# The next pair's queries and keys: load written one tile later and in two transfers

## Chip, cores, metric

One core of one Trainium2 chip. The metric is the device time in microseconds (us) of one execution. The kernel before takes 540.03 us, the median of 3 runs (539.34 to 540.26).

## What is computed

Attention over 4 batches, 8 heads, 576 positions and head width 64, with a rotary turn of queries and keys, and then a mixture of experts in which every token goes to one of 8 experts:

```python
q_rot, k_rot = rotate(q), rotate(k)          # x1*cos - x2*sin, x1*sin + x2*cos
scores = scale * np.matmul(q_rot, k_rot.transpose(0, 1, 3, 2))
attn = softmax(scores)
x = np.matmul(attn, v)                       # tokens of 8*64 = 512
logits, local_gate = x @ w_gate, sigmoid(x @ w_local)
# e = argmax(logits), or the previous token's e when local_gate >= 0.5
h = np.maximum(x[b, s] @ w1[e], 0.0)
out[b, s] = p[e] * (h @ w2[e])
```

## The kernel before, in words

The attention runs over 16 pairs of heads (4 batches with 4 pairs each). A pair has 9 tiles of 128 score rows, so there are 144 steps `g`; `p, i = divmod(g, 9)`. In step `g` TensorE makes the scores of tile `g + 1` (`s`, L266), VectorE takes the minimum of a row (`mn`, L271), ScalarE the exponential (`e`, L288), TensorE turns an earlier tile (`tm` and, for the ninth tile, `tt`), and ScalarE and VectorE split the turned tile into a high and a low part (`pth`, `ptl`). For the pair before, TensorE sums up the values (`pv`, L363). The ninth tile of a pair, made first from pair 2 on, reads `qtail`; the other eight read `qst` and `m`.

What a pair needs is prepared some pairs ahead, on GpSimd (POOL) and by transfers that SyncE (SP) issues:

- `load_qk(p)` (L186 to L188) brings the queries and keys of a pair, each with its turned copy, into `qkl`: four planes of 576 columns, the first two queries, the last two keys. There is one such buffer. From pair 4 on it is written in the program at `i == 0` of pair `p - 3`, behind `rope(p - 1)`, which reads the buffer's earlier contents.
- `rope` (L195, L196): for keys and then for queries, one product with the table, in place, and one sum into `rr`.
- `split_qk` (L205, L206): `rr` is split into `xq` and `xk`, from which SP spreads the pair (`spread`): two transfers of `qtail` (L233), six of `m` (L220 to L222) and four of `qst` (L228), 12 in all, written at `i == 0` ahead of `rope`.
- `split_v` (L211, L212) and `load_v` (L192) do the same for the values.
- Behind each pair come its rows: TensorE multiplies the finished pair with the gate's weights and turns it (`gx`, L437, in two groups), ScalarE and POOL (L444, L450, L451), and for the second group VectorE (L450, L451), scale it into `xrow`, and three row stores (`store`, L461 and L465) bring it to `rows_d` in DRAM, which only the experts read. They are popped from the list `soon` at the end of a step, the stores at `i == 0`, behind `load_qk` in the program.

Buffers that bear on this: `gx` and `pv` share the four PSUM buffers of `ps_t`; `xrow` and the ninth tile's exponentials `et` share the four SBUF buffers of `et_p`, so each of them becomes free when the store has landed, or when `tt` has read it.

From step 12 on TensorE's order is the written one, and a planner puts the instructions of the other engines in order when the program is built, by the order written and by when it reckons that each can go. SP issues in that fixed order, too. Behind the attention, routing and experts follow; all of the first expert work is on the same engines.

Of the kernel before, what the change touches and what calls it, by code (L numbers as in the profile page):

```python
# [136 lines left out]
def tile_attention_moe(ctx, tc, qk, v, tabs, turn, consts, tri, wg, wts, out):  # L137
    nc = tc.nc
    pe, act, dve, pool, sp = nc.tensor, nc.scalar, nc.vector, nc.gpsimd, nc.sync
# [33 lines left out]
    qkl = stage[:, 0:2304].rearrange("p (f s) -> p f s", f=4)  # L173
# [9 lines left out]
    NPAIR = B * NP  # L183
    PASSES = ((0, 0), (0, 1), (1, 0))

    def load_qk(p):  # L186
        b, hp = divmod(p, NP)
        sp.dma_start(qkl, qk[b, hp])  # L188

    def load_v(p):  # L190
        b, hp = divmod(p, NP)
        sp.dma_start(vl[p % 2], v[b, hp])  # L192

    def rope_half(engine, f, x):
        engine.tensor_tensor(x, x, tab[:, 2 * f:2 * f + 2], op=ALU.mult)  # L195
        engine.tensor_tensor(rr[:, f], x[:, 0], x[:, 1], op=ALU.add)  # L196
# [5 lines left out]
    def split_qk(p):  # L202
        parts = [(xq, rr)] if p % 2 == 0 else [(xk[1], rr[:, 1]), (xq[:, :, 0], rr[:, 0])]
        for x, src in parts:
            pool.tensor_scalar(x[:, 0], src, 1.0, 1.0, op0=ALU.mult, op1=ALU.mult)  # L205
            pool.tensor_tensor(x[:, 1], src, x[:, 0].bitcast(F32), op=ALU.subtract)  # L206

    def split_v(p):
        v2 = v2_p.tile([P, 10, 2, D], F32R, tag="v2", name=f"v2_{p}")
        src = vl[p % 2]  # L210
        pool.tensor_scalar(v2[:, :, 0], src, 1.0, 1.0, op0=ALU.mult, op1=ALU.mult)  # L211
        pool.tensor_tensor(v2[:, :, 1], src, v2[:, :, 0].bitcast(F32), op=ALU.subtract)  # L212
        v2_t[p] = v2
# [21 lines left out]
    def spread(p):  # L235
        spread_tail(p)
        spread_k(p)
        spread_q(p)
# [109 lines left out]
    def pv_mm(p, n):  # L348
        u, n = divmod(n, 10)
        h, a = divmod(u, 2)  # L350
        k, hl = divmod(n, 2)
        if n == 0:
            pv_t[p, u] = ps_t.tile([P, HALF], F32, tag="t", name=f"pv_{p}_{u}")
        v2 = v2_t[p]
        hs = slice(h * HALF, (h + 1) * HALF)
        if k < 4:
            lhs = v2[:, 4 * a + k]
            rhs = (pthi, ptlo)[hl][p][:, a, k, hs]
        else:

            lhs = v2[:, 8 + a]
            rhs = (pkhi, pklo)[hl][p][:, hs]
        pe.matmul(pv_t[p, u], lhs.rearrange("p c d -> p (c d)"), rhs, start=(n == 0), stop=(n == 9))  # L363
# [837 lines left out]
    if True:  # L1201
        begin = ExitStack()
        begin.enter_context(tc.manual_schedule())
        raw = pt_p.tile([P, 2, 4, S], F32, tag="pt", name="raw")
        with tc.manual_schedule():
            rest_q, keep_awake, pair_1 = first_pair()
        sp.dma_start(wid, wg)
        load_v(0)
        sp.dma_start(tab[:, 3], tabs[:, 3])
        sp.dma_start(raw[:, 1], qk[0, 2])  # L1210
        sp.dma_start(tab[:, 0:2], tabs[:, 0:2])
        load_v(1)
        sp.dma_start(cst, consts)
        sp.dma_start(trif, tri)

        sp.dma_start(rows_d[0:1], zrow)

        def rope_2():
            for f in (1, 0):
                rope_half(pool, f, raw[:, 1, 2 * f:2 * f + 2])  # L1220

        NSTEP = NPAIR * 9
        soon, todo, minima = [], [], {}
        START = {
            0: [lambda: split_v(0)], 1: [rest_q[1], lambda: keep_awake(1)], 2: [rest_q[2], lambda: load_qk(3)],
            3: [pair_1[0], pair_1[1], rope_2, lambda: split_qk(2)], 4: [pair_1[2]], 5: pair_1[3:5],
            6: pair_1[5:6], 7: pair_1[6:8] + [lambda: split_v(1), lambda: load_v(2)],
            8: [lambda: spread(2)], 40: [lambda: act.copy(trib, trif)],
        }


        cum = [0, *itertools.accumulate(PV_STEPS)]

        def pv_steps(t):
            p, i = divmod(t, 9)
            if 0 <= p < NPAIR:
                for n in range(cum[i], cum[i + 1]):
                    pv_mm(p, n)
                    if n % 10 == 9:
                        pv_evac(p, n // 10)  # L1240

        for g in range(NSTEP):
            if g == GM:
                begin.close()
            with tc.manual_schedule(engines=None if g < GM else MAN0):
                p, i = divmod(g, 9)
                if i == 0 and p % NP == 0:
                    b = p // NP
                    sum_t[b] = sm_p.tile([P, H * NB], F32, tag="sum", name=f"sum_{b}")
                    dve.memset(sum_t[b], 1.0)  # L1250
                mn = minima.pop(g) if g in minima else softmax_min(g)
                if g == 0:
                    rest_q[0]()
                if g + 1 < NSTEP:
                    mm_s(g + 1)
                softmax_exp(g, mn)
                if g < GM - 1:
                    minima[g + 1] = softmax_min(g + 1)
                if g >= 2:
                    tr_main(g - 2)  # L1260
                pv_steps(g - 11)

                if i == 0 and 2 <= p and p + 2 < NPAIR or g == SPREAD_LAST:
                    spread(p + 1)
                if g in START:
                    for f in START[g]:
                        f()
                if i == 0 and 1 <= p and p + 2 < NPAIR:
                    rope(p + 2)
                    if p + 3 < NPAIR:  # L1270
                        load_qk(p + 3)
                if i == 5 and 1 <= p and p + 3 < NPAIR:
                    split_qk(p + 2)
                if g == QK_LAST:
                    split_qk(NPAIR - 1)
                if i == 3 and 1 <= p and p + 1 < NPAIR:
                    split_v(p + 1)
                    if p + 2 < NPAIR:
                        load_v(p + 2)

                if i == GATES_AT.get(p, 7) and p >= 2:
                    soon += gates(p - 2)
                    if (p - 2) % NP == NP - 1:
                        soon.append(lambda b=(p - 2) // NP: scores(b))
                        if (p - 2) // NP == B - 2:
                            todo += route(0, B - 1)
                if soon:
                    soon.pop(0)()
                f = todo.pop(0) if todo else None
                if f:  # L1290
                    list(f())
        moe = experts_phase()
        with tc.manual_schedule(engines=MAN1):
            last = NPAIR - 1
            held = []

            def tail_of(p):
                for n in range(cum[(NSTEP - 12) % 9 + 1], 40):
                    pv_mm(p, n)
                    if n % 10 == 9:  # L1300
                        pv_evac(p, n // 10)

            def pv_unit(u):
                for n in range(10):
                    pv_mm(last, 10 * u + n)
                pv_evac(last, u)

            def first_experts():
                for t in range(1, KE):
                    expert_of(t)  # L1310
                for k in range(2):
                    load_w(1, k)

            def rest_of_w():
                for k in range(LOAD0, 8):
                    load_w(0, k)

            drain = {
                "s": soon, "t": [lambda f=f: list(f()) for f in todo if f], "P": [lambda: tail_of(last - 1)],
                "w": [rest_of_w], "a": [lambda: tr_main(NSTEP - 2)], "b": [lambda: tr_main(NSTEP - 1)],  # L1320
                "g": gates(last - 1), "e": [first_experts], "S": [lambda c=c: split_w(0, c) for c in (1, 2, 3)],
                "u": [lambda u=u: pv_unit(u) for u in range(4)], "x": [lambda: held.append(turn_x(0, True))],
                "G": gates(last), "X": [lambda: held[0]()],
            }
            for c in DRAIN:
                if drain[c]:
                    drain[c].pop(0)()
            assert not any(drain.values())
        with tc.manual_schedule(engines=MAN2):
            side["parts"] = itertools.chain.from_iterable(f() for f in route(B - 1, 1))  # L1330
            for t in moe:
                pe_slot()
                if t == MANUAL:
                    break
        with tc.manual_schedule():
            for t in moe:
                pass
        rest_phase()
# [59 lines left out]
```

## Time and profile before

| | |
|---|---|
| median of 3 runs | 540.03 us |
| the profiled execution | 539.95 us |
| its span, first to last instruction | 538.2 us |
| TensorE matmul busy | 516.9 us (96%) |
| TensorE weight load busy | 458.4 us (85%) |
| VectorE busy | 381.0 us (71%) |
| ScalarE busy | 347.3 us (65%) |
| GpSimd busy | 341.0 us (63%) |
| mean rate of all transfers | 181 GB/s |

The shares are averages over unlike stages. Pairs 2 to 13 of the attention run from about 42 to 243 us, the last pairs with the routing to about 306 us, and the experts from there to about 520 us. In a row of the timeline the first number is the start, the second the duration, and a bracket at its end tells how long the engine had been idle and what ended that.

### The profile page before, as it was taken

The numbers are of one execution on the slowest core, as the hardware profiler recorded it, in microseconds if no ns is written. First come the engines' busy times: TensorE is split into PE (matmuls) and PEld (weight loads), VectorE is DVE, ScalarE is ACT, GpSimd is POOL, SyncE is SP. The second block draws the span as 40 slices with busy tenths as digits, with TensorE's granted clock in tenths as the row PEclk, the third lists the DMA queues.
The fourth block names the chain that finished last, engine by engine and source line by source line (L and its number), as shares of the span: only waits on it lengthen the run. The fifth ranks groups of instructions, "written<-read, shape, count | busy, mean of one in ns | idle before, by whom it ended". The sixth has DMA issues, their size and how long they took to land.

```text
span 538.2 us, 10733 instructions
## 1 busy us (share of the span) xinstructions
PE 516.9 (96%) x3273; PEld 458.4 (85%) x3273; DVE 381.0 (71%) x693; ACT 347.3 (65%) x766; POOL 341.0 (63%) x272
## 2 busy tenths in 40 slices
PE   7998999999999999998989999999999999999993
PEld 4888999999999999998879788887888887888882
DVE  6998999999999999999998845537412746421731
ACT  4988999999999999988776523353433443532440
POOL 4998999979969999896698302346411455411332
PEclk9999999999999999999999999999999999999998
DMA  8659799797996979977378205462537395637350
GB/s 289 265 131 230 197 232 235 186 213 201 221 225 145 230 203 231 222 189 166 57 209 223 76 21 176 148 245 71 205 117 236 98 372 130 223 100 235 82 175 26
DMA packets 63610, 97.34 MB, mean 181 GB/s; under 512 B 28145, under 2 KB 38897, under 8 KB 61746
## 3 DMA queue, kind: packets, MB, share of 16 engines
q1 hardware_dynamic: 60066, 86.45, 59.1%
q0 software_dynamic: 3040, 9.71, 5.6%
q8 instruction: 28, 0.46, 0.4%
q14 instruction: 44, 0.36, 0.2%
q10 hardware_dynamic: 432, 0.36, 0.2%
HBM read 76.95 MB, written 12.86 MB: 167 GB/s over the span
## 4 chain that ended last, share of the span: by engine, by line
PE 80%; DVE 8%; ACT 4%; issue 4%; POOL 2%; DMA 1%; SPq 0%; ACTq 0%; POOLq 0%; DVEq 0%
PE h L959 18%; PE o L1002 17%; PE pv L363 14%; PE s L266 13%; PE tm L324 10%; PE gx L437 3%; DVE mn L271 2%; PE th L993 2%; PE tx L945 1%; ACT e L288 1%; DVE ptl L306 1%; PE tk L334 1%; DVE w L904 1%; DMA turn<-in_turn_dram 1%; ACT w L901 1%
## 5 line engine op out<-in xcount | busy, mean ns | idle before, releaser
L1002 PE MATMUL o<-w,hs 128*128 128x512 f32 x456 | 113.4, 398 | 0.0
L271 DVE TENSOR_REDUCE mn<-s 128x1 f32<-128x576 f32 x144 | 107.2, 745 | 2.3 <-PE s L266 0.9
L959 PE MATMUL h<-w,xs 128*128 128x512 f32 x444 | 106.2, 393 | 0.8 <-DVE xs L306 0.5
L288 ACT ACTIVATE e<-s,mn 128x576 f32<-128x576 f32 x128 | 95.4, 745 | 15.9 <-DVE mn L271 13.3
L306 DVE TENSOR_TENSOR ptl<-tm,pth 128x512 fp32r<-128x512 f32 x139 | 95.4, 687 | 13.4 <-ACT pth L302 8.9
L1008 POOL DMA_INDIRECT out_dram<-os,sidx x19 | 23.1, 1214 | 126.5 <-ACTq L910 85.0
L266 PE MATMUL s<-m,qst 128*128 128x288 f32 x512 | 96.3, 310 | 5.7 <-ACT e L288 4.8
L959 PEld LDWEIGHTS h<-w,xs 128*128 128x128 f32 x444 | 82.5, 188 | 19.1 <-DVE w L904 1.1
L1002 PEld LDWEIGHTS o<-w,hs 128*128 128x128 f32 x456 | 83.0, 188 | 17.4 <-DVE hs L984 0.4
L302 ACT CAST pth<-tm 128x512 fp32r<-128x512 f32 x139 | 80.8, 582 | 10.6 <-PE tm L324 9.6
L266 PEld LDWEIGHTS s<-m,qst 128*128 128x128 f32 x512 | 74.1, 188 | 10.0 <-ACT e L288 7.5
L363 PE MATMUL pv<-pth,v 128*128 128x288 f32 x256 | 76.6, 315 | 1.3 <-DVE ex_row L702 0.4
L324 PE MATMUL tm<-wid,e 128*128 128x128 f32 x512 | 77.0, 272 | 0.0
L363 PE MATMUL pv<-ptl,v 128*128 128x288 f32 x256 | 76.3, 314 | 0.0
L195 POOL TENSOR_TENSOR stage<-stage 128x1152 f32<-128x1152 f32 x26 | 69.2, 2670 | 3.0 <-DMA stage<-in_qk_dram 2.9
L324 PEld LDWEIGHTS tm<-wid,e 128*128 128x128 f32 x512 | 62.2, 140 | 0.7 <-DVE ptl L306 0.3
L904 DVE TENSOR_TENSOR w<-stage,w 128x1024 fp32r<-128x1024 f32 x37 | 50.6, 1403 | 14.6 <-ACT w L901 9.7
L363 PEld LDWEIGHTS pv<-pth,v 128*128 128x128 f32 x256 | 48.3, 189 | 3.6 <-issue 2.5
L363 PEld LDWEIGHTS pv<-ptl,v 128*128 128x128 f32 x256 | 48.3, 189 | 0.0
L306 DVE TENSOR_TENSOR xs<-tx,xs 128x512 fp32r<-128x512 f32 x19 | 13.1, 689 | 42.7 <-ACTq L910 32.9
L196 POOL TENSOR_TENSOR stage<-stage 128x576 f32<-128x576 f32 x26 | 37.1, 1434 | 0.3
L306 DVE TENSOR_TENSOR hs<-th,hs 128x512 fp32r<-128x512 f32 x26 | 17.5, 687 | 27.7 <-ACTq L910 16.2
(201 smaller groups left out, 821.3 us busy)
## 6 DMA issues: line engine op xcount, KB each, us to landing
stage<-in_wts_dram SPq DMA_DIRECT2D x84, 512.0 KB
stage<-in_qk_dram SPq DMA_DIRECT2D x13, 1152.0 KB
qst<-xq SPq DMA_DIRECT2D x56, 128.0 KB
stage<-in_v_dram SPq DMA_DIRECT2D x16, 320.0 KB
m<-xq SPq DMA_DIRECT2D x14, 288.0 KB
m<-xk SPq DMA_DIRECT2D x14, 288.0 KB
m<-xq SPq DMA_DIRECT2D x14, 256.0 KB
m<-xk SPq DMA_DIRECT2D x14, 256.0 KB
```

What stands on the lines that cost most here:

```text
L195: engine.tensor_tensor(x, x, tab[:, 2 * f:2 * f + 2], op=ALU.mult)
L196: engine.tensor_tensor(rr[:, f], x[:, 0], x[:, 1], op=ALU.add)
L266: pe.matmul(st[:, h, lo:hi], lhs, keys[:, k0:k0 + hi - lo], start=(n == 0), stop=(n == len(parts_) - 1))
L271: dve.tensor_reduce(mn, s_t[g][:, :, 0:HALF], axis=AX.XY, op=ALU.min)
L288: act.activation(dst.rearrange("p (h s) -> p h s", h=2), s_t.pop(g)[:, :, 0:HALF], AF.Exp, bias=mn, scale=-1.0, accum_out=sums[:, col:col ...
L302: act.copy(hi, src)
L306: dve.tensor_tensor(lo, src, hi.bitcast(F32), op=ALU.subtract)
L324: pe.transpose(ps[:, k], src[:, k * P:(k + 1) * P], ident)
L363: pe.matmul(pv_t[p, u], lhs.rearrange("p c d -> p (c d)"), rhs, start=(n == 0), stop=(n == 9))
L904: (pool if k in on_pool else dve).tensor_tensor(lo, src, hi.bitcast(F32), op=ALU.subtract)
L959: pe.matmul(ps[:, c], xs_t[t][:, x, k], w[y][:, c * 512:(c + 1) * 512], start=(k == 0 and n == 0), stop=(k == 3 and n == 2))
L1002: pe.matmul(ps, hs_t[t][:, x, k], w[y][:, (k % 2) * 512:(k % 2 + 1) * 512], start=(k == 0 and n == 0), stop=(k == 7 and n == 2))
```

## The change

`load_qk` issues two transfers in place of one, the two planes of the keys first and then those of the queries, and from pair 4 on the call stands at `i == 1` in place of `i == 0`. As the row stores are popped at the end of step `i == 0`, the load is now behind them in the program. The load of pair 3, in step 2, stays where it is and is two transfers too.

```diff
     def load_qk(p):
         b, hp = divmod(p, NP)
-        sp.dma_start(qkl, qk[b, hp])
+        for f in (1, 0):
+            sp.dma_start(qkl[:, 2 * f:2 * f + 2], qk[b, hp, :, 2 * f:2 * f + 2])
...
                 if i == 0 and 1 <= p and p + 2 < NPAIR:
                     rope(p + 2)
-                    if p + 3 < NPAIR:
-                        load_qk(p + 3)
+                if i == 1 and 1 <= p and p + 3 < NPAIR:
+                    load_qk(p + 3)
                 if i == 5 and 1 <= p and p + 3 < NPAIR:
                     split_qk(p + 2)
```

## Rows read from the trace of the kernel before

**Rows 1.** Busy time by stretch: length, PE, PEld, DVE, ACT, POOL, PEclk, DMA share, GB/s

```profile
0.00:13.50 13.50, 10.42 (x43) 6.28 (x44) 9.03 (x27) 5.65 (x13) 6.24 (x10) 1.00 0.86 288
...
102.80:119.50 16.70, 16.70 (x133) 16.51 (x132) 15.83 (x32) 15.51 (x41) 13.68 (x11) 1.00 0.92 215
...
169.60:186.30 16.70, 16.57 (x131) 16.09 (x131) 15.46 (x30) 15.37 (x39) 16.38 (x16) 1.00 0.96 227
...
253.10:280.00 26.90, 24.91 (x184) 22.15 (x182) 26.30 (x61) 20.18 (x48) 19.78 (x30) 1.00 0.56 117
```

**Rows 2.** Chain that ended last, first scores of a pair: start, us, what

```profile
108.59 0.80 PE s L266 x6
...
124.97 0.80 PE s L266 x6
...
141.34 0.80 PE s L266 x6
...
158.04 0.80 PE s L266 x6
...
224.85 0.80 PE s L266 x6
```

**Rows 3.** TensorE's weight loads: one idle time, and the waits from 137 to 236 us

```profile
149.22 0.19 PEld L363 LDWEIGHTS pv<-pth,v 128*128 128x128 f32 x1 [0.33 <-issue]
...
PEld pv L363 <- issue: 1.6, 5, 0.3
PEld tm L324 <- DVE ptl L306: 1.2, 6, 0.2
PEld pv L363 <- POOL v L211: 0.3, 1, 0.3
```

**Rows 4.** Timeline ahead of that idle time, VectorE and TensorE

```profile
145.77 0.18 DVE L450 TENSOR_TENSOR gm<-gx,sum 128x36 f32<-128x36 f32 x1
...
148.32 0.27 PE L340 MATMUL tt<-wid,et 128*128 128x128 f32 x1
...
148.69 0.41 DVE L451 TENSOR_TENSOR xrow<-gx,sum 128x256 f32<-128x256 f32 x1
```

**Rows 5.** The same two VectorE instructions two pairs earlier

```profile
113.03 0.18 DVE L450 TENSOR_TENSOR gm<-gx,sum 128x36 f32<-128x36 f32 x1
113.13 0.41 DVE L451 TENSOR_TENSOR xrow<-gx,sum 128x256 f32<-128x256 f32 x1
```

**Rows 6.** Timeline of SP's transfers around one load

```profile
171.27 3.08 SPq L228 DMA_DIRECT2D qst<-xq  x4
175.45 0.34 SPq L188 DMA_DIRECT2D stage<-in_qk_dram  x1
175.89 0.38 SPq L461 DMA_DIRECT2D rows_d<-xrow  x1
...
176.88 0.73 SPq L461 DMA_DIRECT2D rows_d<-xrow  x1
...
180.06 1.29 SPq L233 DMA_DIRECT2D qtail<-xq  x2
```

**Rows 7.** Busy time by stretch around that load, columns as in rows 1

```profile
174.90:176.40 1.50, 1.50 (x14) 1.50 (x14) 1.50 (x4) 1.44 (x5) 1.50 (x2) 1.00 0.46 105
176.40:180.70 4.30, 4.30 (x36) 4.25 (x35) 3.44 (x8) 3.97 (x11) 4.14 (x7) 1.00 0.97 304
```

**Rows 8.** Timeline of POOL: the keys' sum, then the queries' sum

```profile
169.32 1.44 POOL L196 TENSOR_TENSOR stage<-stage 128x576 f32<-128x576 f32 x1
...
173.96 1.46 POOL L196 TENSOR_TENSOR stage<-stage 128x576 f32<-128x576 f32 x1
```

**Rows 9.** Waits of SP and of POOL: us in total, times, longest

```profile
SPq L188 <- POOL stage L196: 12.8, 9, 2.2
...
POOL stage L195 <- DMA stage<-in_qk_dram: 2.9, 3, 2.2
...
POOL xq L205 <- DMA qst<-xq: 2.6, 2, 1.8
```

**Rows 10.** TensorE's weight loads: the first use of a spread pair

```profile
226.83 0.30 PEld L266 LDWEIGHTS s<-m,qst 128*128 128x128 f32 x2 [0.22 <-issue]
```

## Prediction

> **What bounds the kernel now.** I read the busy time by stretch first, with one stretch for each pair of the attention. Through the attention TensorE is busy 16.70 of 16.70 us or a little less, at a granted clock of 1.00, which is the higher level of 2.4 GHz; GpSimd and the transfers stand close behind it: 16.38 of 16.70 us and a transfer share of 0.96 in the stretch from 169.60 us [rows 1]. So TensorE sets the pace, and a wait that is taken from GpSimd or from a transfer is worth something only where TensorE then waits less. The second view is therefore the chain that ended last, at the first scores of each pair. The early pair from 108.59 us takes 124.97 - 108.59 = 16.38 us. The pair from 141.34 us takes 16.70, and the four from 158.04 to 224.85 us take 66.81 / 4 = 16.70 [rows 2]. TensorE has the same products to make in all of them, so five pairs are each 0.32 us longer than need be.
>
> The third view, the idle times of the weight loads, says where these 0.32 us are. In every late pair `pv` at L363 starts 0.33 us late: five times 'issue', 1.6 us in all, and once under another name, 0.3 us [rows 3]. The fourth, the timeline just ahead, tells who is late: VectorE's L451, which empties a `gx` buffer of the PSUM pool that `pv` needs next. It ends at 148.69 + 0.41 = 149.10 us, 0.12 us ahead of the delayed `pv` [rows 3, 4]. Its neighbour L450, which reads the same `gx`, went at 145.77, so L451 stood back for 2.9 us. In the earlier pair it follows L450 after 0.10 us [rows 5], and there nothing waits. It starts 0.10 us after `tt` has ended (148.32 + 0.27 = 148.59) [rows 4], and `tt` is the last reader of `et`, with which `xrow` shares four buffers. I read this so: when the planner placed L451, the buffers that the row stores of the pair before hold were not free by its reckoning, so L451 got the buffer of `et` and a place behind `tt`.
>
> Why are the row stores late? SP's timeline: the spread's last transfers end their issue at 171.27 + 3.08 = 174.35 us, then SP stands until the load goes at 175.45, and only behind it go the three stores, from 175.89 to 177.61 [rows 6]. The load waited for GpSimd's last sum, which ends at 173.96 + 1.46 = 175.42 [rows 8]; SP stands so nine times, 12.8 us in all [rows 9]. And the stores' data queue behind the load's: the transfers are less than half busy before it (0.46, 174.90 to 176.40), then run at 304 GB/s for 4.30 us until 180.70 [rows 7]. A store that could have gone at 174.35 therefore moves its data after 180.7.
>
> **The change, part by part.**
>
> *Stores ahead of the load.* They need `xrow`, which is ready long before: L451 ends 149.10 - 141.34 = 7.8 us into its pair, SP is through with the spread 174.35 - 158.04 = 16.3 us into the pair [rows 2, 4, 6]. So they go when SP comes free, about 1.5 us earlier at this load, and their data land in the half-empty stretch and not behind 4.3 us of load: 4 to 5 us earlier. The next pair's L451 would come at 175.4 + 4.4, so near 180 us (its place behind the pair's first scores as in rows 2 and 4: 145.77 - 141.34 = 4.4). That is between the two landings, about 178 after the change and about 182 before. This is what makes me think that L451 can move back behind L450. Worth: six waits of `pv`, 0.33 us each: 2.0 us. The `tm` waits of 0.2 us in the same six pairs [rows 3] I count at nothing extra: the pair is longer by 0.32 us and not 0.53 [rows 2].
>
> *The load one step later.* Where GpSimd's sum is the releaser, the queries' half waits for the same sum as before (175.42) and goes at about 176.3 in place of 175.45: three stores (175.89 to 177.61, 1.7 us) started at 174.35 end at 176.1. That is 0.9 us later. The keys' half needs only the keys' sum, 169.32 + 1.44 = 170.76 [rows 8], and so goes straight behind the stores. At loads where SP and not GpSimd was late, both halves go up to 1.7 us later. Cover: GpSimd begins the next pair with the keys, whose half takes about half of 4.3 us, so it lands about 2.2 - 1.7 = 0.5 us earlier than before in the worst case, and the queries' product comes one product later. I take this part at nothing; without that cover it costs up to 1.7 us, once and not for each pair, unless it adds to itself from pair to pair.
>
> *Two transfers.* One more issue of SP, 0.34 + 0.1 us gap [rows 6], 13 times, where SP stands anyway: nothing. The rate of smaller transfers is bounded by two rows: 288 GB/s in the start, where none is over 576 KB, but TensorE's start is in it, and 304 for the whole load [rows 1, 7]. 1152 KB is 1.18 MB: 4.1 against 3.9 us, so 0.2 us for a load at most, and below nothing is not likely, since nothing is left out. I take 0.1 us, hidden. GpSimd's waits for the load, 2.9 us in three places, 2.2 us of it in one [rows 9], go away, and so GpSimd is ahead early; TensorE did not wait there, so I count nothing.
>
> The Trainium skill speaks against the split: "DMA: Bandwidth & Descriptors", section Bandwidth, wants transfers of 1 MiB or more, and its Anatomy section has a fixed cost of about 2.0 us for one. By that, as an estimate from the page, a split load would take up to 2.0 us more where nothing overlaps, and the slower rival below would be the likelier one. The start of this trace, at 288 GB/s with smaller transfers queued behind one another [rows 1], does not agree that the fixed cost adds up.
>
> *What is late next.* When TensorE runs 0.33 us faster in a pair, the spread has to keep up. It barely does now: at 226.83 the first scores from `qst` wait 0.22 us for nothing named, which I read as that transfer [rows 10], the 12 transfers of the spread having ended just before. GpSimd waits 2.6 us twice for the `qst` transfers to have read `xq` [rows 9], in just these pairs. With the stores moved into the half-empty stretch the transfers behind the load begin some 0.8 us earlier (1.5 us at 0.46 busy leaves 0.8 free [rows 7]), for each such pair, and part of GpSimd's 2.6 us goes. I count 0.2 us gained (rows 10) and 0.2 us given back over all: nothing.
>
> *Sum.* 2.0 us from six waits. Behind the attention VectorE bounds the stage from 253 to 280 us (26.30 of 26.90) [rows 1], and it starts when the scores come, so what is gained ahead passes on. The profiled execution took 539.95 us, 0.08 below the median: 540.0 - 2.0 = 538.0 us.
>
> **The rivals.**
>
> *L451 stays where it is (or GpSimd and the transfers take the place of the wait).* The planner sees other durations than the chip; if the stores were not its reason, the 0.33 us stay. Or the spread is ready no earlier, and the `pv` wait becomes a `qst` wait of the same size, for which rows 10 speak. Then the time is 540.0 less rows 10's 0.2: 539.8 us, within 0.7 us each way.
>
> *Slower: the load comes too late.* One place: the queries' half behind three stores. If a store in the written order is not ready when SP is (SP holds all that is behind it, the load, the values and the next spread), the load goes later by more than its cover of 0.5 us; GpSimd, busy 16.38 of 16.70 us [rows 1], cannot make it up; the spread comes later and TensorE waits for `qst`, where it has no slack now [rows 10]. It decides once the delay passes about 0.5 us; the price is up to 1.7 us of stores and 0.2 of slower halves: 540.0 + 1.7 = 541.7 us, 541.1 to 543.
>
> *More gained.* If GpSimd, freed of 2.9 + 2.6 us of waits [rows 9], and VectorE's order in the last pairs also bring the stage from 253 to 280 us forward (TensorE idle for 2.0 of 26.90 us there [rows 1]), another 2 us go: 536.0 us.
>
> That nothing is done at all is no case: SP must issue two transfers, and later.
>
> **How the numbers follow.** Forecast 538.0 (536.8 to 538.9): 0.45. More gained: 0.10. No difference: 0.27. Slower: 0.18. A measurement of this kernel tells about 0.2% (1.1 us) from no change, so faster is 0.45 less 0.02 for its upper end and 0.10: 0.53; within 0.2% 0.29; slower 0.18. The likeliest case is 538.0. The range goes from 536.2, which leaves half of the larger gain out (0.05), to 541.4, which leaves most of the slower case out (0.12).
>
> **What would show it.** In the profile after: SP's order is spread, three stores, two loads; L451 within 0.2 us of L450 in the late pairs; no idle time ahead of `pv`; pairs of 16.4 us in the chain up to 225 us, and the mark of 224.85 us at about 223. GpSimd's waits for the load are gone. I am wrong if L451 still follows `tt`; if idle times ahead of `s` from `qst` appear; or if the pairs get shorter and the stretch from 243 to 306 us longer, by another order of VectorE's work.

## The result and the profile after

The changed kernel takes **545.52 us** (median of 11 runs, 541.65 to 549.49), the kernel before 540.03 in as many runs (539.08 to 541.27). The ratio is 1.0102, interval 1.0080 to 1.0124: 1.0% slower, outside the forecast's range and of the other sign. The runs of the changed kernel spread over 8 us, those of the kernel before over 2. The profiled execution took 548.22 us, span 546.4, against 539.95 and 538.2.

All line numbers behind 188 are one higher than before: the load is L189, GpSimd's product and sum L196 and L197, the splits L206 and L207, the row scaling L451 and L452, the row stores L462 and L466.

**SP does what the diff says, and the load goes late.** First SP's transfers around one load, before and then after (start, duration, line, transfer):

```profile
67.01 3.11 SPq L228 DMA_DIRECT2D qst<-xq  x4
70.23 0.52 SPq L188 DMA_DIRECT2D stage<-in_qk_dram  x1
70.85 0.39 SPq L461 DMA_DIRECT2D rows_d<-xrow  x1
```

```profile
70.59 0.53 SPq L462 DMA_DIRECT2D rows_d<-xrow  x1
71.17 0.47 SPq L466 DMA_DIRECT2D rows_d<-xrow  x1
72.94 0.40 SPq L462 DMA_DIRECT2D rows_d<-xrow  x1
73.38 1.53 SPq L189 DMA_DIRECT2D stage<-in_qk_dram  x2
```

The load goes 3.15 us later (73.38 against 70.23). Two stores take 1.1 us; then SP stands from 71.64 to 72.94 for the third one, and behind it stands the load. The third store is that of GpSimd's own rows, and GpSimd's timeline after shows when these are ready, and its wait for the load:

```profile
72.07 0.84 POOL L452 TENSOR_TENSOR xrow<-xrow,sum 128x384 f32<-128x384 f32 x1
...
79.60 2.67 POOL L196 TENSOR_TENSOR stage<-stage 128x1152 f32<-128x1152 f32 x1 [2.21 <-DMA stage<-in_qk_dram]
```

72.07 + 0.84 = 72.91: the store goes 0.03 us later. At 79.60 GpSimd has waited 2.21 us for the load; before, its product at this place waited for 0.13 us.

SP stands so for GpSimd's rows at this load and, for 1.6 us, at the next one. At the third it does not: the rows were ready at 101.55 us, the three stores go one behind another from 106.11 us, and the load is later still. First the load before, then the third store and the load after:

```profile
102.65 1.85 SPq L188 DMA_DIRECT2D stage<-in_qk_dram  x1
```

```profile
107.26 0.52 SPq L462 DMA_DIRECT2D rows_d<-xrow  x1
107.83 0.98 SPq L189 DMA_DIRECT2D stage<-in_qk_dram  x2
```

The three loads go 3.15, 4.04 and 5.18 us later than before, while TensorE is ahead of before by up to 0.78 us. At the third, the three stores make up 1.7 us of it; the other 3.5 us have come round: the spread ahead of them ends its issue at 106.02 us in place of 102.55. So the delay adds to itself from pair to pair.

GpSimd's waits over the whole run (us in total, times, longest):

```profile
POOL gm L451 <- ACT xrow L445: 8.6, 5, 3.6
POOL stage L196 <- DMA stage<-in_qk_dram: 7.7, 6, 2.6
```

The wait for the load was 2.9 us [rows 9] and is 7.7; the prediction had it gone.

**What was to be gained was gained, but for two waits of 0.2 us.** The chain of waits at the first scores of a pair, then TensorE's weight loads and VectorE's row scaling at the places that answer to [rows 3 to 5]:

```profile
130.28 0.80 PE s L267 x6
146.63 0.79 PE s L267 x6
163.00 0.80 PE s L267 x6
```

```profile
153.30 0.14 PEld L341 LDWEIGHTS tt<-wid,et 128*128 128x128 f32 x1
153.50 0.19 PEld L364 LDWEIGHTS pv<-pth,v 128*128 128x128 f32 x1
```

```profile
151.07 0.18 DVE L451 TENSOR_TENSOR gm<-gx,sum 128x36 f32<-128x36 f32 x1
151.17 0.41 DVE L452 TENSOR_TENSOR xrow<-gx,sum 128x256 f32<-128x256 f32 x1
```

The pairs take 16.35 and 16.37 us where [rows 2] had 16.70, VectorE's second row instruction is 0.10 us behind the first, and no bracket stands at this `pv`; from 137 to 243 us two waits of 0.2 us at `pv` are left. TensorE's own order differs here, too. Before, four scores `s` went between `tt` (148.22 us) and the delayed `pv` (149.22); now `pv` goes straight behind `tt`, and the scores follow at 154.14. It is so in six late pairs, so the words ahead of the prediction that TensorE's order is the written one do not hold for both kernels at this place.

**Where it was lost, first place: about 6 us in pair 6.** GpSimd, VectorE and TensorE from 111 to 118 us, after:

```profile
111.43 0.28 POOL L451 TENSOR_TENSOR gm<-xrow,sum 128x54 f32<-128x54 f32 x1
113.67 2.63 POOL L196 TENSOR_TENSOR stage<-stage 128x1152 f32<-128x1152 f32 x1 [1.96 <-DMA stage<-in_qk_dram]
116.26 0.83 POOL L452 TENSOR_TENSOR xrow<-xrow,sum 128x384 f32<-128x384 f32 x1
```

```profile
112.69 0.75 DVE L272 TENSOR_REDUCE mn<-s 128x1 f32<-128x576 f32 x1
117.17 0.09 DVE L1251 MEMSET sum<- 128x40 f32 x1 [3.73 <-POOL xrow L452]
```

```profile
117.87 0.18 PEld L341 LDWEIGHTS tt<-wid,et 128*128 128x128 f32 x1 [3.35 <-DVE ptl L307]
```

Read it from below. TensorE's weight loads stand 3.35 us for `ptl`, an instruction that VectorE has queued behind a memset. That memset clears the row sums of a batch; they live in a tile of two buffers, so the one for the third batch needs the one of the first, which GpSimd's L452 still reads. And in the new order of GpSimd the keys' product (L196, 2.63 us) stands between L451 and L452, and waits 1.96 us for the late load. The sums are those of pair 8, whose scores begin at 146.63 us; the memset only happens to stand there in VectorE's fixed order. Before, it went at 114.17 us without a wait.

Behind this idle time the granted clock is at the lower of its two levels, 1.2 GHz. Busy time by stretch, columns as in [rows 1]:

```profile
117.80:122.00 4.20, 4.12 (x17) 3.90 (x18) 3.38 (x8) 1.56 (x5) 4.20 (x4) 0.50 1.06 213
122.00:126.00 4.00, 4.00 (x26) 3.98 (x26) 2.76 (x5) 2.82 (x7) 4.00 (x7) 0.73 0.73 159
126.00:130.00 4.00, 4.00 (x35) 4.00 (x34) 3.63 (x7) 3.72 (x9) 3.57 (x2) 1.00 0.92 309
```

At 0.50 and 0.73 TensorE gets through 4.20 × 0.50 + 4.00 × 0.73 = 5.0 us of work at full clock in 8.2 us: some 3 us more.

**Second place: the late pairs wait for the spread.** TensorE's weight loads, the first use of `qst` in three late pairs:

```profile
198.37 0.56 PEld L267 LDWEIGHTS s<-m,qst 128*128 128x128 f32 x4 [0.59 <-ACT pth L303]
...
215.30 0.57 PEld L267 LDWEIGHTS s<-m,qst 128*128 128x128 f32 x4 [0.51 <-ACT pth L303]
...
233.67 0.56 PEld L267 LDWEIGHTS s<-m,qst 128*128 128x128 f32 x4 [1.96 <-ACT sum L429]
```

The names in these brackets are engines long done; what these products need is the spread. They read the pair's first head, which is complete with the third of the four `qst` transfers; by the trace's landings that one was there at 198.20, 215.08 and 233.46 us, 0.17 to 0.22 us ahead of the three rows. In the second of them the product behind the weights names it:

```profile
215.33 0.77 PE L267 MATMUL s<-m,qst 128*128 128x288 f32 x4 [0.33 <-DMA qst<-xq]
```

Where [rows 10] had 0.22 us (its third transfer landed at 226.66), 3.06 us stand now.

The difference, from TensorE's products one by one (the n-th after against the n-th before, us; the place is the time in the trace of before):

| place | after - before | what lies ahead of it |
|---|---|---|
| 58.9 | -0.33 | start (+0.39 in e4, which has the order of before) |
| 108.4 | -0.78 | one `pv` wait of 0.3 gone, as in e4 |
| 120 | +5.40 | 3.35 idle, and the lower clock |
| 191.3 | +4.56 | `pv` waits gone |
| 208.0 | +4.86 | 0.59 for `qst`, `pv` wait gone |
| 242.9 | +6.50 | 0.51 and 1.96 for `qst`, `pv` waits gone |
| 306 | +6.55 | the last pairs and routing: nothing |
| last | +6.85 | the experts: 0.3 |

TensorE is 5.30 us behind at 141 us; the new waits for `qst` add 3.06 - 0.22 = 2.84; it is 6.50 behind at 242.9. So 1.64 us were gained in the late pairs, where the `pv` waits were. The rest of the span's difference (8.2 less 6.85) lies behind the start of TensorE's last product, where the span goes on for 10.9 us against 9.5 before. e1, which has the load in the same place, has 9.5 there, and e4, which has the order of before, 10.2, so I don't put it down to the change.

### The profile page after: what moved, and what is told of

It is laid out like the page before. It is cut to its first block, busy times and chain, and to the rows that moved or that the text cites. A ratio compares the mean times of both kernels' runs of the same rounds, so it can differ in the third digit from the quotient of the medians.

```text
span 546.4 us, 10731 instructions
## 1 busy us (share of the span) xinstructions
PE 519.1 (95%) x3273; PEld 461.5 (84%) x3273; DVE 379.7 (69%) x693; ACT 346.8 (63%) x766; POOL 342.2 (63%) x272
## 4 chain that ended last, share of the span: by engine, by line
PE 63%; DVE 9%; POOL 7%; DMA 6%; ACT 5%; issue 5%; SPq 2%; ACTq 0%; POOLq 0%; DVEq 0%
PE h L960 18%; PE o L1003 17%; PE pv L364 9%; PE s L267 8%; PE tm L325 6%; DVE mn L272 3%; POOL stage L196 2%; PE gx L438 2%; ACT e L289 2%; PE th L994 2%; DVE ptl L307 2%; PE tx L946 1%; DMA m<-xk 1%; POOL xq L207 1%; DMA qst<-xq 1%
## 5 line engine op out<-in xcount | busy, mean ns | idle before, releaser
L196 POOL TENSOR_TENSOR stage<-stage 128x1152 f32<-128x1152 f32 x26 | 69.4, 2669 | 7.7 <-DMA stage<-in_qk_dram 7.7
L197 POOL TENSOR_TENSOR stage<-stage 128x576 f32<-128x576 f32 x26 | 37.1, 1426 | 0.9
```

## The experiments

The questions: is it the place or the split? Is it one place, the memset (theory A), or loads that come late everywhere (theory B)? Which of the three stores holds the load? And could the forecast 2.0 us be had at all? The kernel before took 540.64 us beside e1 to e4, 540.15 beside e5 to e9 and 540.6 beside e10 to e13; the ratios are to these.

**e1: the place alone.** The changed kernel with one transfer.

```diff
-        for f in (1, 0):
-            sp.dma_start(qkl[:, 2 * f:2 * f + 2], qk[b, hp, :, 2 * f:2 * f + 2])
+        sp.dma_start(qkl, qk[b, hp])
```

> The place alone: one transfer, written at step i == 1 behind the row stores. Theory A (the loss is one place: GpSimd's product of the keys, which waits for the late half load, stands between the two row instructions of pair 7, and VectorE's clearing of the sums waits for the second): here the planner keeps the two row instructions together, so no idle time over 1 us ahead of TensorE's tt near 118 us; 538.5 to 540.5 us. Rival B (the loss is that the load comes later and the spread of the late pairs with it): the load is as late as in the change, so TensorE waits for qst in pairs 10 to 13 and the time is 542 us or more. Rival C (halves are slower transfers): no halves here, so about the time before.

Measured: 544.42 us (542.14 to 546.01), 1.0067 [1.0042, 1.0091]. GpSimd's waits for the load between 50 and 250 us, the longest of them, and two of TensorE's waits:

```profile
POOL stage L195 <- DMA stage<-in_qk_dram: 11.3, 4, 5.8
```

```profile
82.89 5.31 POOL L195 TENSOR_TENSOR stage<-stage 128x1152 f32<-128x1152 f32 x2 [5.78 <-DMA stage<-in_qk_dram]
```

```profile
162.81 0.56 PEld L266 LDWEIGHTS s<-m,qst 128*128 128x128 f32 x4 [1.94 <-ACT sum L428]
...
231.75 0.56 PEld L266 LDWEIGHTS s<-m,qst 128*128 128x128 f32 x4 [1.94 <-ACT sum L428]
```

The place alone costs most of it: 3.8 us. The memset stall is only 1.42 us here, TensorE's idle time there 1.05, and the clock stays at 1.00. TensorE is 0.70 us behind before at 141 us and 4.59 at 242.9; what is lost between lies in `qst` waits (the third transfer landed at 162.59 and 231.55 us, 0.2 us ahead of the rows shown). So theory A, as the whole cause, falls. SP's standing for GpSimd's rows is not needed for the loss either: here the three stores around 71 us go without it (70.97, 71.55 and 72.13 us), and the load goes at 72.70, 2.47 us later than before. The split softens the wait for the load (keys' half first: 7.7 us in place of 11.3), but it puts the keys' product between GpSimd's two row instructions.

**e2: the split alone.** The kernel before with two transfers, in the old place.

```diff
-        sp.dma_start(qkl, qk[b, hp])
+        for f in (1, 0):
+            sp.dma_start(qkl[:, 2 * f:2 * f + 2], qk[b, hp, :, 2 * f:2 * f + 2])
```

> The split alone: two transfers, keys first, at step i == 0 ahead of the row stores. Theory A: in this program the product stands between the row instructions in another pair than the one whose sums are cleared, so TensorE's 3 us idle time is not there: 539 to 541 us. Rival B: load not later, so no loss: 539 to 540.5. Rival C (halves are slower by a fixed cost of up to 2 us each, 13 loads on a path with little slack): 543 us or more, and GpSimd's waits for the load of 7 us or more.

Measured: 540.01 us (539.06 to 541.17, 12 runs), 0.9992 [0.9978, 1.0005]: no change. The estimate of the prediction from the Trainium skill, "DMA: Bandwidth & Descriptors", sections Bandwidth and Anatomy, of up to 2.0 us for each split load is not borne out: 13 loads are split here, and the upper end of the interval leaves 0.3 us for all of them. The Anatomy section gives its 2.0 us for transfers issued by GpSimd; these are issued by SP. The late pairs keep their wait, and VectorE its gap of 2.9 us:

```profile
148.39 0.19 PEld L364 LDWEIGHTS pv<-pth,v 128*128 128x128 f32 x1 [0.33 <-issue]
```

```profile
144.96 0.18 DVE L451 TENSOR_TENSOR gm<-gx,sum 128x36 f32<-128x36 f32 x1
...
147.86 0.42 DVE L452 TENSOR_TENSOR xrow<-gx,sum 128x256 f32<-128x256 f32 x1
```

So the `pv` waits hang on the order of stores and load, and not on the size of a transfer.

**e3: without the memset's wait.** The changed kernel with four buffers of sums, so that the third batch's memset needs no earlier one.

```diff
-                    sum_t[b] = sm_p.tile([P, H * NB], F32, tag="sum", name=f"sum_{b}")
+                    sum_t[b] = sm_p.tile([P, H * NB], F32, tag="sum", name=f"sum_{b}", bufs=4)
```

> The change, with four buffers for the softmax sums in place of two, so that the clearing at the start of a batch waits for no reader. GpSimd's order is that of the change. Theory A: the idle time near 118 us and the lower clock behind it go, worth about 6 us of the profile of the change: 538 to 541 us, with a spread between runs as small as before (2 us). Rival B: the waits for qst stay and the time stays at 543 us or more. Rival C: no difference to the change, 545 us.

**e4** is the same edit on the kernel before, as control.

> Control: the kernel before with four buffers for the sums; the order on every engine is the same but for the place of waits. All theories: 539.5 to 540.5 us, no difference, since TensorE has no wait there before.

Measured: e4 540.65 us, 1.0004 [0.9989, 1.0019]: nothing. e3 543.87 us (542.22 to 546.98), 1.0070 [1.0042, 1.0098]. The stall and the lower clock are gone from e3's profile (its difference to before is -0.74 us at 120 and -0.17 at 141, where the change had +5.40 and +5.30), and yet only 1.7 us of the median, and the intervals of the two kernels overlap. What stands in their place:

```profile
POOL stage L196 <- DMA stage<-in_qk_dram: 12.1, 8, 3.5
```

```profile
210.70 0.56 PEld L267 LDWEIGHTS s<-m,qst 128*128 128x128 f32 x4 [1.09 <-ACT xrow L445]
...
228.28 0.56 PEld L267 LDWEIGHTS s<-m,qst 128*128 128x128 f32 x4 [1.16 <-ACT xrow L445]
```

At 262 us this kernel is 3.43 us behind before. I read it so: while TensorE lost 6 us, GpSimd and the transfers caught up; without that stop GpSimd waits 12.1 us for the loads in place of 7.7, and the late pairs wait for it. The two places of the loss are not two sums to be added: the first pays for part of the second.

**e8: GpSimd's store behind the load.** The changed kernel; the store of GpSimd's rows is popped one step later, the two others stay ahead of the load.

```diff
-        return [sums, lambda: rows(0, 3), last_rows]
+        return [sums, lambda: rows(0, 3), lambda: rows(3, 2), pool_store]
```

> The change, but with GpSimd's row store (the third) behind the load; VectorE's two stores stay ahead of it. Theory D (the load is late because SP stands at the store whose rows GpSimd has still to scale, and holds the load behind it): the loads go 1 to 3 us earlier in pairs 4 to 7, GpSimd's waits for the load fall from 7.7 us to under 4, and the time falls to 540 to 542 us. Rival E (three issues of SP, 1.6 us, and the stores' data ahead of the load are the cause): only a third of that goes, the time stays at 543 us or more.

Measured: 544.99 us (541.75 to 548.08), 1.0081 [1.0051, 1.0110].

```profile
POOL gm L451 <- ACT xrow L445: 10.5, 6, 3.5
POOL stage L196 <- DMA stage<-in_qk_dram: 2.9, 3, 1.3
```

The waits for the load fall from 7.7 to 2.9 us, as expected. The time does not follow: GpSimd now waits for ScalarE's rows (10.5 us against 8.6), and the memset stalls again (TensorE idle for 1.87 us). The loads go 0.81, 0.05 and 2.63 us earlier than in the change at the three places above, where 1 to 3 us were expected. The wait moved on, and the expected time was missed.

**e9: all three stores behind the load.** The changed kernel, with the stores of VectorE's rows put off as well. This was meant to be e2 by SP's order. The last steps are those of e8.

```diff
-            if engine is pool:
+            if engine is pool or p < POOL_ROWS:
                 stores.append(lambda: store(j0, n, xr))
```

> The change, with all three row stores behind the load, which stays at step i == 1 and in two transfers. If being behind the stores is the whole loss, this is the split alone again: 539.5 to 540.5 us, GpSimd's waits for the load about 1 us, and pv late by 0.33 us in the late pairs as before. If the later step itself costs, 542 us or more.

Measured: 548.58 us (547.04 to 550.16), 1.0154 [1.0126, 1.0183]. The worst of all, and not the time of e2, as was expected.

```profile
176.26 1.29 SPq L462 DMA_DIRECT2D rows_d<-xrow  x2
177.60 0.52 SPq L466 DMA_DIRECT2D rows_d<-xrow  x1
```

```profile
184.70 0.42 DVE L452 TENSOR_TENSOR xrow<-gx,sum 128x256 f32<-128x256 f32 x1 [1.74 <-DMA rows_d<-xrow]
```

```profile
185.24 0.19 PEld L364 LDWEIGHTS pv<-pth,v 128*128 128x128 f32 x1 [2.16 <-issue]
...
221.10 0.19 PEld L364 LDWEIGHTS pv<-pth,v 128*128 128x128 f32 x1 [2.82 <-POOL v L212]
```

Here VectorE waits for row stores to land before it may write `xrow`, and `pv` waits 2 to 3 us for the PSUM buffer: the buffers of [rows 3, 4], at six to nine times the wait. SP's order is not that of e2. The edit puts GpSimd's rows, the largest of the three stores, first; in e2 they go last. By the trace's landings GpSimd's store landed at 184.61 us, and VectorE's row instruction goes at 184.70; at the second wait it is 220.44 and 220.56. In e2 all three stores of that pair were there at 182.18. So e9 says what another order of the stores costs, and nothing on the load's step. Why its spread of pair 3 is already through SP about 3 us later than in e2 stays open.

**e5 and e6: the forecast gain without the late load.** The kernel before, and e2, with VectorE's rows in a buffer that is not shared with `et`.

```diff
-            xr = et_p.tile([P, S], F32, tag="et", name=f"xrow_{p}_{j0}")
+            xr = xt_t[p] if j0 else et_p.tile([P, S], F32, tag="et", name=f"xrow_{p}_{j0}")
```

> The kernel before, with VectorE's scaled rows written into the first columns of the pair's own xt, which nothing reads any more, in place of a buffer of et_p. The load stays where it was. This parts the gain of the change from its loss. If the 0.33 us of pv per late pair come from the shared buffers, L451 follows L450 in all pairs without any change to the load, pairs 5 to 13 take 16.4 us and the time is 537.5 to 539 us. If GpSimd and the transfers stand right behind TensorE, the pairs get waits for qst of the same size and the time is 539.5 to 540.5 us.

> As the one before, and the load in two transfers at step i == 0, ahead of the row stores. The split alone left the spread of pairs 3 to 9 landing 5 to 8 us ahead of its use, so what GpSimd lacks should be less: 536.5 to 538.5 us if waits of pv were the only loss; 539 us or more if the late pairs then wait for qst.

Measured: e5 541.64 us (539.69 to 543.53), 1.0018 [1.0004, 1.0031]; e6 541.45, 1.0028 [1.0013, 1.0042]. There is a small loss, where the gain or, for e5, at worst 539.5 to 540.5 us was expected. By TensorE's products e5 is 0.68 us ahead of before at 174.6 us: the `pv` waits are gone, in a kernel whose load order is the old one, which shows that the shared buffer was the reason for them. Then it is given back, at first uses of `qst` (the third transfer landed at 176.31 and 210.98 us):

```profile
176.41 0.57 PEld L266 LDWEIGHTS s<-m,qst 128*128 128x128 f32 x4 [0.57 <-ACT pth L302]
...
211.08 0.56 PEld L266 LDWEIGHTS s<-m,qst 128*128 128x128 f32 x4 [1.77 <-ACT et L288]
```

At 210 us e5 is 1.20 us behind before, at 262 us 2.07; but its profile is of its slowest run (543.53 us). That of e6 took 540.67: 1.17 us ahead at 208 us, 0.11 ahead at 210, 0.53 behind at 262. So neither kernel gets the 2.0 us of the forecast, though the load keeps its old place in both. I read it so that GpSimd comes behind TensorE by less than those 2 us; e13 measures it.

**e13: does GpSimd set the end of the attention?** The kernel before; GpSimd makes one instruction of the values' split twice in three late pairs: 3 × 1.57 = 4.7 us more for GpSimd, nothing for any other.

```diff
-        pool.tensor_tensor(v2[:, :, 1], src, v2[:, :, 0].bitcast(F32), op=ALU.subtract)
+        for _ in range(2 if 10 <= p <= 12 else 1):
+            pool.tensor_tensor(v2[:, :, 1], src, v2[:, :, 0].bitcast(F32), op=ALU.subtract)
```

> The kernel before with GpSimd's second value product (L212, 1.57 us) done twice in pairs 10 to 12: the same numbers again, 4.7 us more of GpSimd's time, off the path from load to spread, and nothing else. Theory G (GpSimd's chain of work sets the end of the attention, with little slack): its last split of queries and keys ends 2 to 4.7 us later and the time rises by as much, 542 to 545 us. Rival P (TensorE sets the pace, GpSimd has slack): 540 to 541 us.

Measured: 543.92 us (542.92 to 546.67), 1.0067 [1.0042, 1.0092]: 3.3 us of 4.7. One TensorE wait carries it:

```profile
229.48 0.57 PEld L267 LDWEIGHTS s<-m,qst 128*128 128x128 f32 x4 [2.88 <-issue]
```

Up to there TensorE is where it was before to 0.02 us (at 226 us). So GpSimd has some 1.4 us in hand in the late pairs; by the interval it is anything from nothing to 2.4. The last split of GpSimd, in before, after and e13:

```profile
245.93 1.40 POOL L206 TENSOR_TENSOR xq<-stage,xq 128x576 fp32r<-128x576 f32 x1
```

```profile
252.49 1.55 POOL L207 TENSOR_TENSOR xq<-stage,xq 128x576 fp32r<-128x576 f32 x1
```

```profile
249.64 1.53 POOL L206 TENSOR_TENSOR xq<-stage,xq 128x576 fp32r<-128x576 f32 x1
```

It ends at 247.33, 254.04 and 251.17 us; TensorE's 2000th product, in the first routing, comes at 275.98, 282.57 and 279.00. In all 14 kernels of this case it lies 27.8 to 30.1 us behind that split's end. That alone does not say which of the two waits for the other; e13, where only GpSimd got more to do, does.

**e10, e11, e12: GpSimd relieved.** All rows are scaled by VectorE and ScalarE, in the kernel before (e10), in the changed kernel (e11) and in e6 (e12).

```diff
-POOL_ROWS = 11
+POOL_ROWS = 0
```

> The kernel before with all rows scaled by VectorE: GpSimd loses two instructions per pair (1.1 us, eleven pairs) and its waits for ScalarE's copy of them (6.8 us); VectorE gets about 0.6 us more per pair, ScalarE 0.5 us less. Theory G: GpSimd's last split ends 3 to 10 us earlier, TensorE becomes the bound, 536 to 539 us. Rival P: VectorE's extra work makes TensorE wait, 541 us or more.

> The change with all rows scaled by VectorE: no store then waits for GpSimd, no instruction of GpSimd stands between two others waiting for a load, and VectorE's clearing of the sums waits for no GpSimd row. Theory G and D together: the loss goes, 536 to 540 us, and the load's place behind the stores costs little. If the late load is itself the loss: 541 us or more, with GpSimd waiting 5 us or more for loads.

> All three that help one engine: the load split at step i == 0, VectorE's second group of rows in xt, all rows scaled by VectorE. Theory G: TensorE alone bounds the attention, every pair 16.4 us, 535 to 538 us, faster than both kernels. Otherwise 539 us or more.

Measured, 12 runs each: e10 539.38 us, 0.9977 [0.9964, 0.9990]; e11 **539.02 us** (538.02 to 540.50), 0.9968 [0.9957, 0.9980]; e12 539.04, 0.9972 [0.9960, 0.9983]. e11 holds the changed lines as they are, and beats both kernels. GpSimd's waits for the load in e11 and the stretch from 50 to 250 us:

```profile
POOL stage L196 <- DMA stage<-in_qk_dram: 13.8, 8, 3.2
```

```profile
50.00:250.00 200.00, 197.65 (x1548) 193.92 (x1545) 191.73 (x380) 178.42 (x443) 173.61 (x121) 1.00 0.82 210
```

GpSimd waits 13.8 us for loads, more than e1's 11.3, and it costs nothing: GpSimd has 173.61 us of work in these 200, where before it had 183.68. The same lines that cost 1.0% with the rows on GpSimd cost nothing without them (e11 against e10). In the early pairs the load is as late as in the change (74.00 and 106.72 us against 73.38 and 107.83); in the late ones it has caught up (207.83 against 215.80, and 208.87 before). The edit takes away GpSimd's work, the store that SP stands for and the memset's wait for GpSimd all at once, so it does not say which of them counts.

The price of the relief is in the early pairs, where VectorE is now the busier (191.73 of 200 us): at 141 us e11 is 1.26 us behind before, at 262 us 1.47 ahead. Here expectations were missed. In e10 GpSimd's last split ends at 247.53 us, no earlier than before (247.33), where 3 to 10 us earlier was expected, and e10 and e12 are slower than the 536 to 539 and 535 to 538 us that theory G had for them. With less work on GpSimd the end of the attention is not set by GpSimd alone.

## Why the prediction was wrong, step by step

**"So TensorE sets the pace, and a wait that is taken from GpSimd or from a transfer is worth something only where TensorE then waits less": this step failed as the ground for counting the later load at nothing.** It was read from busy time, 16.70 against 16.38 us [rows 1]. But GpSimd was busy for 183.68 of the 200 us from 50 us on, before the change, and waited in most of the rest. A wait put into its chain (load, product and sum, splits, spread) comes out at TensorE some pairs later, less what GpSimd has in hand, about 1.4 us (e13). The rule works for gains as it was put; for losses it had to be asked of GpSimd as well. The Trainium skill, "Perfetto Trace Analysis", section Identifying the Most-Contended Engine, picks the engine with the highest occupancy, but judges TensorE's headroom by the busy share of its weight loads, or by the work done against the peak, and not by the busy time of its products. In the stretch from 169.60 us the weight loads are busy for 16.09 us and GpSimd for 16.38 [rows 1], so read in that way GpSimd comes first there, and e13 agrees.

**"They need `xrow`, which is ready long before": failed.** This looked at VectorE's L451, 7.8 us into its pair [rows 4]. There are three stores, and one is of GpSimd's rows, which were ready at 72.91 us where SP asked for them at 71.64. The prediction's own rival, "if a store in the written order is not ready when SP is", is what happened at this load and the next. GpSimd's L451 does not stand in the prediction; but it would have looked safe there. In the trace of before it ends at 70.78 us at this place, ahead of SP's third store (71.87). It came late by the new order that the planner made for GpSimd.

**"I take this part at nothing; without that cover it costs up to 1.7 us, once and not for each pair": mis-sized.** The first of these loads came 3.15 us later where 0.9 to 1.7 were reckoned, as SP also stands for the third store. The cover of 0.5 us was right in kind (the split cuts GpSimd's waits for the load from 11.3 to 7.7 us, e1 against the change), too small in size. And it is not once: the next two loads came 4.04 and 5.18 us later. A later load makes the split and the spread later, and by SP's order the next stores and the next load. The prediction named this ("unless it adds to itself from pair to pair") and gave it no price. The slower rival had the right mechanism and the right place of the end (`qst`, [rows 10]); its deciding point of 0.5 us was not measured, and its price of 1.7 us was 3.8 us for the place alone (e1) and 5.5 with the split.

**Not foreseen: another engine's wait on GpSimd.** I named what is queued behind the load on SP, not what is queued behind GpSimd's row instructions: VectorE's memset, behind it `ptl`, and TensorE. With the clock this makes 6 us in the profiled run, which is one of the slower ones (548.22 us). By e3 it is worth about 1.7 us of the median, a difference that the two intervals don't set clear of nothing; as I read it, GpSimd catches up meanwhile.

**"Worth: six waits of `pv`, 0.33 us each: 2.0 us": right as a term, wrong in the sum.** 1.64 us were gained in the late pairs, and e2 and e5 bear out the reading of VectorE's order from the shared buffer. But "what is late next" was counted at nothing, and there it went: e5 loses the `pv` waits too and ends 1.5 us slower than before (by its interval 0.2 to 1.7). One reading there was loose: GpSimd's 2.6 us of waiting for `qst` is the total of two waits [rows 9], and not "2.6 us twice"; no sum uses it twice.

**Right:** SP's order; L451 back behind L450; pairs of 16.35 us; the split at no cost (e2); nothing new in the stretch behind the attention (6.50 us behind at 242.9, 6.55 at 306) and in the experts. The signs to be wrong by had been named: idle times ahead of `s` from `qst` did appear.

**Open:** why the runs of the change spread so far. The five slowest of 11 (546.7 to 549.5 us) have a mean clock of 0.986 to 0.988, the six others (541.7 to 545.5) 0.991 to 0.996. That would fit a stall at the memset which now and then ends in a lower clock, but only one execution was profiled, and the memset can't be the whole of it: e3, where it waits for nothing, still spreads from 542.2 to 547.0 us, with 0.989 in its slowest run and 0.995 in its fastest.

## What to carry to other kernels

Before a transfer is moved behind others on a queue that issues in order, find the instruction that makes each of those others ready, on its own engine, and compare its end with the moment at which the queue comes free: the last one decides, not the typical one. Do it in the order that the planner makes for the changed kernel: in the trace of before the row that came late here was early enough. Before a gain is counted, ask how far behind the second engine is: double an instruction of it in one stretch and see how much comes out at the end; what doesn't come out is its slack, and more than that is hardly gained while its work stays the same. If the second engine is the limit, take work from it first, and the order of transfers may stop to matter, as in e11.

## What the runs showed of the hardware

The granted clock behind an idle time of TensorE was not the same for idle times of like length. After 3.35 us (the change, 114.5 to 117.9 us) it was 0.50 up to 124 us, 0.96 from 124 to 126 us, and 1.00 from then on. After 2.82 us in e9 it fell too:

```profile
221.00:226.00 5.00, 4.87 (x26) 4.88 (x27) 4.19 (x8) 2.11 (x5) 5.00 (x4) 0.66 0.98 216
```

After 2.88 us in e13 (at 229.48 us) it stayed at 1.00 over the next 10.6 us, and so it did after the 1.96 us of the changed kernel at 233.67 us; yet behind the 1.87 us of e8 (at 116.51 us) it was 0.56 over 118 to 120 us and 0.58 over 120 to 122, and 1.00 again from 122 us. What makes the difference these runs don't tell.
